# First two tiles of r and k by the sync queue in fp32, GpSimd's loads behind the masks, and another order: an RWKV-6 and mixture-of-adapters kernel

## The chip, the cores and the metric

One core of a Trainium2 chip runs the kernel. The metric is the device time of one execution in microseconds. Besides TensorE (PE, with its weight loads as PEld), the core has VectorE (DVE), ScalarE (ACT), GpSimd (POOL) and the sync engine (SP), and 16 DMA engines that all queues share. Each engine takes its instructions strictly in the order in which the program lists them.

## The reference

Two stages. A recurrence over 768 steps for 4 sequences of 8 heads with 48 features, then for each of the 3,072 rows a mixture of 8 low-rank adapters, of which the two with the largest logits count.

```
for t in range(S):
    cur = einsum('bhd,bhe->bhde', u * k[t], v[t])
    y[t] = einsum('bhd,bhde->bhe', r[t], state + cur)
    state = w[t][..., None] * state + einsum('bhd,bhe->bhde', k[t], v[t])

logits = x @ w_gate                      # x = y as (3072, 384)
top 2 of 8 experts, softmax over the two
out = x + sum over the two of weight * ((x @ A[e]) @ B[e])
```

## The kernel before

Work is cut into 24 tiles of 128 steps, six to each sequence; all 8 heads (384 columns) of a tile go together. Within a tile the recurrence is written as matrix products. A triangular matmul adds up log w (`cs`, `ci`), two exponentials turn the sums into factors (`grow`, `exps`), `mult` scales r and k by them, `tr` transposes both on PE, `trev` takes the result out of PSUM, `amm` forms the 128 x 128 products of r and k for each head, and `aev` masks them. `kv` adds to the state, which `sev` copies out. `ymm` makes the tile's output from state and masked products. The direct term of u is made apart: `rkp` multiplies r by k, `xk` and `xkev` transpose that (together with the output of a tile three earlier), `dgmm` and `dgev` give one number for each head and row, and `dv` multiplies v by it. `xev` adds `dv` and `ymm`'s result.

The second stage works in batches of four tiles (the last ones are of three and one): `lgmm` and `gate` for the logits, `gmax`, `gsel` and `gmul` for the weights, `zmm`, `zw`, `zT` and `zTev` for the low-rank middle, and for each tile `dmm`, `oev` and `store`. The name with a number, as in `mult.0`, is a stage and its tile; `xk.-3` is one that holds `rkp.0` alone.

The order is written out by hand in the string `ORDER` (lines 36 to 76): a list of stage and tile, which fixes the sequence of every engine's queue. Each stage's engine is fixed as well, or picked for each tile by the strings in `ENGINES` (lines 79 to 87: A is ACT, D is DVE, P is GpSimd; the string of `xkev` begins with tile -3).

Loads go by two queues. The sync queue carries w (in fp32: tile 0 and tile 1 apart, then pairs of tiles), the packed weights, the adapters' B, r and k of tile 0 in fp32 (`rk_first`), and the stores. The GpSimd queue carries the rest of r and k (`load_rk`, in groups of 1, 2 or 4 tiles) and v (`load_v`), and turns them into fp16 on the way. GpSimd also makes the masks: `strict` and the identity in `begin()`, `rest` and `at_mask` in `masks` (line 243). `rest` is first used by `cs.1`, `at_mask` by `aev.0`. `warm` issues matmuls whose result isn't used.

The engines' queues around the start, as `ORDER` gives them (before):

```
SP    w.0 rk.0 | w.1 weights moe_B w.2 w.4 w.6 ...
POOL  strict identity | rk.1 rk.2 v.0 v.1 rk.4 rk.6 masks v.4 rk.8 v.8 rk.12 v.12 dv.0 ...
ACT   ln.0 grow.0 exps.0 xkev.-3 ln1.0 cast16 grow.1 trev.0 xkev.-2 casts ...
DVE   rkp.0 rkp.1 mult.0 rkp.2 rkp.3 aev.0 mult.1 sev.0 xev.0 mult.2 aev.1 ...
```

Of the kernel before, what the change touches and what calls it, by code (L numbers as in the profile page):

```python
# [41 lines left out]
xkev.0 grow.3 dgmm.3 lgmm.0 aev.1 ci.3 sev.1 trev.2 ymm.1 exps.3 kv.2 cs.4 amm.2 ln.6 sev.2 xev.1 mult.3 tr.3 aev.2
kv.3 sev.3 dgev.3 grow.4 rkp.4 trev.3 ci.4 load_w.14 rkp.5 ymm.2 exps.4 ln.8 cs.5 amm.3 xk.1 grow.5 ci.5 mult.4 tr.4
xkev.1 dv.2 aev.3 exps.5 dgmm.4 ymm.3 cs.6 xev.2 ln.10 dv.3 rkp.6 load_w.16 grow.6 trev.4 mult.5 rkp.7 xk.2 xev.3
ci.6 amm.4 xkev.2 tr.5 xk.3 exps.6 cs.7 trev.5 load_v.16 aev.4 xkev.3 grow.7 amm.5 dgmm.5 lgmm.1 lgmm.2 dgmm.6
lgmm.3 ci.7 mult.6 tr.6 exps.7 aev.5 mult.7 trev.6 ymm.4 kv.4 cs.8 tr.7 amm.6 gate.3 grow.8 ln.12 ci.8 sev.4 ymm.5
exps.8 load_v.20 dgev.5 dv.4 trev.7 gmax.3 dv.5 xev.4 kv.6 cs.9 xk.4 gsel.3 aev.6 gmul.3 xev.5 zmm.3 grow.9 xkev.4
ci.9 amm.7 lgmm.4 dgmm.7 exps.9 cs.10 zw.3 rkp.8 dgev.7 rkp.9 mult.8 xk.5 sev.6 zT.3 dv.6 xkev.5 ymm.6 zTev.3
grow.10 tr.8 trev.8 aev.7 dv.7 dgmm.8 xev.6 dmm.0 ci.10 lgmm.5 kv.7 amm.8 ymm.7 xk.6 rkp.10 aev.8 xev.7 mult.9 oev.0
sev.7 store.0 ln.14 load_w.18 dmm.1 xkev.6 exps.10 kv.8 cs.11 xk.7 rkp.11 tr.9 mult.10 rkp.12 oev.1 grow.11 xkev.7  # L50
dgmm.9 ymm.8 ci.11 lgmm.6 lgmm.7 trev.9 exps.11 dgmm.10 gate.7 dgev.9 amm.9 tr.10 cs.12 sev.8 dmm.2 kv.9 aev.9
rkp.13 ln.16 dv.8 trev.10 sev.9 xev.8 gmax.7 mult.11 gsel.7 ymm.9 xk.8 dv.9 rkp.14 amm.10 gmul.7 kv.10 tr.11 xev.9
grow.12 ci.12 oev.2 xkev.8 aev.10 zmm.7 trev.11 zw.7 xk.9 exps.12 dmm.3 lgmm.8 dgmm.11 store.1 cs.13 amm.11 ymm.10
oev.3 xkev.9 zT.7 grow.13 sev.10 dgev.11 mult.12 tr.12 ci.13 lgmm.9 zTev.7 dgmm.12 rkp.15 kv.12 dmm.4 store.2
load_w.20 dv.10 aev.11 store.3 exps.13 cs.14 xev.10 ymm.11 dv.11 trev.12 oev.4 mult.13 xk.10 xev.11 dmm.5 grow.14
amm.12 ci.14 tr.13 store.4 ln.18 rkp.16 xkev.10 xk.11 lgmm.10 aev.12 exps.14 dgmm.13 mult.14 dgev.13 cs.15 trev.13
sev.12 ymm.12 dv.12 amm.13 oev.5 tr.14 kv.13 grow.15 xkev.11 lgmm.11 ci.15 dmm.6 trev.14 aev.13 gate.11 exps.15
amm.14 cs.16 rkp.17 sev.13 grow.16 xev.12 oev.6 xk.12 gmax.11 mult.15 zmm.11 gsel.11 aev.14 store.5 dv.13 ci.16
xkev.12 gmul.11 dgmm.14 tr.15 ymm.13 dgmm.15 dmm.7 kv.14 lgmm.12 ln.20 exps.16 trev.15 cs.17 dgev.15 zw.11 zT.11
store.6 amm.15 mult.16 xev.13 tr.16 oev.7 grow.17 sev.14 load_w.22 ci.17 zTev.11 rkp.18 xk.13 dv.14 exps.17 dv.15  # L60
rkp.19 xkev.13 trev.16 dmm.8 ymm.14 aev.15 cs.18 dgmm.16 oev.8 lgmm.13 grow.18 kv.15 amm.16 xev.14 ln.22 ci.18 xk.14
ymm.15 xkev.14 mult.17 aev.16 xev.15 dmm.9 tr.17 dmm.10 sev.15 dgmm.17 lgmm.14 exps.18 kv.16 trev.17 sev.16 cs.19
ymm.16 oev.9 mult.18 oev.10 grow.19 dgev.17 amm.17 ci.19 aev.17 rkp.20 dv.16 xev.16 xk.15 tr.18 exps.19 mult.19
rkp.21 xkev.15 cs.20 kv.18 xk.16 lgmm.15 dgmm.18 trev.18 grow.20 ymm.17 gate.15 ci.20 tr.19 xkev.16 dgmm.19 amm.18
gmax.15 dv.17 rkp.22 xev.17 exps.20 trev.19 gsel.15 gmul.15 dgev.19 mult.20 zmm.15 cs.21 sev.18 dv.18 grow.21 xk.17
store.7 lgmm.16 rkp.23 xkev.17 store.8 dmm.11 aev.18 kv.19 amm.19 lgmm.17 zw.15 sev.19 ci.21 zT.15 oev.11 exps.21
ymm.18 tr.20 dgmm.20 aev.19 zTev.15 dv.19 cs.22 dmm.12 trev.20 xev.18 ymm.19 dmm.13 amm.20 kv.20 mult.21 oev.12
grow.22 ci.22 oev.13 exps.22 xk.18 tr.21 xkev.18 xev.19 trev.21 xk.19 aev.20 cs.23 mult.22 store.9 dgmm.21 dgev.21
xkev.19 amm.21 dv.20 grow.23 sev.20 tr.22 store.10 lgmm.18 store.11 ymm.20 trev.22 ci.23 dmm.14 exps.23 oev.14
lgmm.19 aev.21 kv.21 amm.22 dmm.15 dv.21 gate.19 sev.21 xev.20 mult.23 store.12 xk.20 oev.15 xkev.20 gmax.19 aev.22  # L70
ymm.21 tr.23 dgmm.22 zmm.19 lgmm.20 dgmm.23 trev.23 kv.22 amm.23 gsel.19 sev.22 xev.21 xk.21 gmul.19 ymm.22 dgev.23
# [495 lines left out]
```

## Time and profile before

| what | value |
|---|---|
| median of 3 runs | 100.42 us (99.06 to 101.35) |
| the profiled execution | 100.22 us |
| its span in the profile | 98.5 us |
| PE busy, share of the span | 82.8 us, 84% |
| DVE busy | 79.0 us, 80% |
| ACT busy | 69.0 us, 70% |
| POOL busy | 49.2 us, 50% |
| moved by the GpSimd queue (loads) | 6.88 MB written, 41.7% of 16 engines' span |
| moved by the sync queue (loads and stores) | 10.25 MB, 31.5% |

The span runs from the first to the last instruction of one profiled execution; what lies around it belongs to the time as well. A row of the timeline gives start, duration, engine, line, operation, output and inputs with shapes, a count where neighbours were merged, and in brackets the idle time of the engine just before and what ended it. Busy time is what the profile shows as running; a matmul's end is modelled, and a PE that is busy all the time is not PE at its peak.

### The profile page before, as it was taken

The page shows a single profiled execution, that of the slowest core. Times are in us where ns is not written, and L with a number is a line of the kernel's source. Part 1 is how long each engine was busy: PE and PEld are TensorE (multiplying, and loading weights), DVE is VectorE, ACT ScalarE, POOL GpSimd, SP SyncE. Part 2 cuts the span into 40 slices and gives each one's busy share as a digit, 9 for nine tenths or more (in the row PEclk, how much of TensorE's full clock was granted, in tenths as well). Part 3 has the DMA queues.
Part 4 walks back from the last instruction along what each step waited for, and adds up shares of the span by engine and source line. Part 5 has one row for each costly group of instructions (what it writes and reads, how often), then busy time and mean ns, then how long its engine had stood idle before and what let it go on. Part 6 is the DMA issues. An engine that isn't in the chain of part 4 may idle for free.

```text
span 98.5 us, 3274 instructions
## 1 busy us (share of the span) xinstructions
PE 82.8 (84%) x1326; PEld 60.6 (62%) x1326; DVE 79.0 (80%) x165; ACT 69.0 (70%) x162; POOL 49.2 (50%) x77
## 2 busy tenths in 40 slices
PE   3871778897678998899998989999999999989730
PEld 2230536575356876767885867788787687957310
DVE  5514227679999989899999999999989999986610
ACT  5433346777957797879886978899886779655450
POOL 6997144600970087926757364773639306070100
PEclk9998555599999999999999999999999999999998
DMA  2999999999999999999999313522400240402644
GB/s 60 259 195 234 272 277 260 261 270 271 264 253 215 209 205 213 208 210 251 271 223 307 137 48 114 164 80 87 160 7 0 80 156 10 160 10 80 237 166 159
DMA packets 13439, 17.34 MB, mean 176 GB/s; under 512 B 880, under 2 KB 13296, under 8 KB 13424
## 3 DMA queue, kind: packets, MB, share of 16 engines
q0 software_dynamic: 6256, 6.88, 41.7%
q1 hardware_dynamic: 7168, 10.25, 31.5%
q8 instruction: 10, 0.16, 0.7%
q14 instruction: 5, 0.04, 0.1%
HBM read 19.29 MB, written 4.72 MB: 244 GB/s over the span
## 4 chain that ended last, share of the span: by engine, by line
PE 48%; DVE 25%; issue 7%; DMA 7%; ACT 5%; POOL 2%; ACTq 1%; POOLq 0%; DVEq 0%
PE trp L331 10%; DVE at L352 7%; DMA rk<-in_rk_dram 7%; PE xk_ps L398 6%; PE a_ps L346 5%; DVE rk L297 5%; DVE xs L389 4%; PE s_ps L363 3%; PE y_ps L383 3%; PE d_ps L496 3%; PE cs_ps L280 3%; PE cs_ps L289 3%; DVE zw L470 3%; PE cs_ps L281 3%; PE y_ps L377 2%
## 5 line engine op out<-in xcount | busy, mean ns | idle before, releaser
L322 POOL TENSOR_TENSOR dv<-v,dg 128x384 f32<-128x384 f16 x24 | 20.3, 862 | 22.7 <-DVE dg L255 11.5
L352 DVE TENSOR_TENSOR at<-a_ps,at_mask 128x1024 f16<-128x1024 f32 x24 | 29.2, 1216 | 2.4 <-PE a_ps L346 2.2
L331 PE MATMUL trp<-ident,rk 128*128 128x128 bf16 x192 | 15.6, 227 | 2.8 <-DVE rk L297 2.8
L285 ACT ACTIVATE e<-cs_ps 128x384 bf16<-128x384 f32 x24 | 12.0, 499 | 6.7 <-PE cs_ps L281 5.5
L305 POOL TENSOR_TENSOR rkp<-rk 128x384 f16<-128x384 f16 x14 | 13.3, 954 | 6.4 <-PE xk_ps L398 3.7
L331 PEld LDWEIGHTS <-rk 128*128 128x128 bf16 x192 | 12.2, 101 | 5.4 <-DVE rk L297 4.1
L297 DVE TENSOR_TENSOR rk<-rk,e 128x768 bf16<-128x768 f16 x23 | 14.5, 630 | 1.0 <-ACT e L293 1.0
L259 ACT COPY rkT<-trp 128x512 f32<-128x512 f32 x22 | 13.0, 591 | 2.1 <-PE trp L331 2.1
L293 ACT ACTIVATE e<-cs_ps 128x384 bf16<-128x384 f32 x24 | 11.8, 493 | 3.8 <-PE cs_ps L289 3.6
L389 DVE TENSOR_TENSOR xs<-dv,y_ps 128x384 f16<-128x384 f32 x24 | 13.1, 544 | 0.7 <-POOL dv L322 0.6
L259 ACT COPY xkT<-xk_ps 128x384 f32<-128x384 f32 (+1 forms) x25 | 11.2, 450 | 3.3 <-PE xk_ps L398 3.1
L346 PE MATMUL a_ps<-rkT 48*128 48x128 bf16 x192 | 10.0, 225 | 0.5 <-ACT rkT L259 0.3
L398 PE MATMUL xk_ps<-ident,rkp 128*128 128x128 f16 x72 | 8.4, 228 | 2.3 <-DVE rkp L305 2.3
L268 ACT ACTIVATE logw<-w_in 128x768 f16<-128x768 f32 x11 | 9.3, 848 | 0.0
L383 PE MATMUL y_ps<-v,at 128*128 128x48 f16 x192 | 8.8, 185 | 0.6 <-DVE at L352 0.6
L346 PEld LDWEIGHTS <-rkT 48*128 48x128 bf16 x192 | 5.9, 97 | 4.9 <-issue 1.5
L289 PE MATMUL cs_ps<-logw,ident 128*128 128x384 f16 x24 | 8.3, 346 | 0.5 <-ACT e L285 0.5
L281 PE MATMUL cs_ps<-logw,strict 128*128 128x384 f16 x24 | 8.3, 348 | 0.2 <-ACT logw L266 0.2
L398 PE MATMUL xk_ps<-ident,xs 128*128 128x128 f16 x72 | 8.2, 223 | 0.4 <-DVE xs L389 0.4
L253 ACT CAST S_sb<-s_ps 128x384 bf16<-128x384 f32 x15 | 7.4, 490 | 1.5 <-DVE dg L255 0.5
L496 PE MATMUL d_ps<-Ball,zT 128*128 128x384 f16 x24 | 7.8, 326 | 0.6 <-ACT zT L259 0.6
L502 ACT COPY res<-d_ps 128x384 f32<-128x384 f32 x13 | 6.1, 485 | 2.5 <-PE d_ps L496 2.3
(74 smaller groups left out, 158.6 us busy)
## 6 DMA issues: line engine op xcount, KB each, us to landing
out_dram<-res SPq DMA_DIRECT2D x24, 192.0 KB, 2.1
w_in<-in_w_dram SPq DMA_DIRECT2D x11, 384.0 KB, 14.1
...
v<-in_v_dram POOLq DMA_DIRECT2D x1, 288.0 KB, 12.1
```

The lines of the kernel that those rows point to most:

```text
L259: nc.scalar.copy(out=out.bitcast(F32), in_=in_.bitcast(F32))
L285: nc.scalar.activation(out=e2[:, 0], in_=cs_ps[:, 0:HD], func=ACT.Exp)
L293: nc.scalar.activation(out=st[t]["e2"][:, 1], in_=cs_ps[:, 0:HD], func=ACT.Exp, scale=-1.0)
L297: nc.vector.tensor_mul(rk2.rearrange("s m p h d -> s (m p h) d")[:, :, 0:D], st[t]["rk"].rearrange("s m (h d) -> s (m h) d", d=D), st[t][" ...
L305: (nc.gpsimd if ENGINES["rkp"][t] == "P" else nc.vector).tensor_mul(p_, st[t]["rk"][:, 0], st[t]["rk"][:, 1])
L322: nc.gpsimd.tensor_mul(dv_, st[t]["v16"], st[t]["dg"].rearrange("p (h o) -> p h o", o=1).to_broadcast([L, H, D]))
L331: nc.tensor.transpose(trp[:, m, p, :], rk2[:, m, p, :, :].rearrange("s a b -> s (a b)"), ident)
L346: nc.tensor.matmul(a_ps[:, g, p, :], lhsT=rkT[base:base + D, 1, p, :], rhs=rkT[base:base + D, 0, p, :], start=True, stop=True)
L352: nc.vector.tensor_mul(at, st[t]["a_ps"].rearrange("s g p f -> s (g p) f"), at_mask.to_broadcast([128, H, 128]))
L383: nc.tensor.matmul(y_ps[:, h, :], lhsT=d["at"][:, g * P + p, :], rhs=d["v16"][:, h, :], start=(c == 0 and h == 0), stop=(h == H - 1), skip ...
L389: nc.vector.tensor_add(xs, st[t]["dv"].rearrange("p a b -> p (a b)"), st[t]["y_ps"].rearrange("p a b -> p (a b)"))
L398: nc.tensor.transpose(xk_ps[:, 3 * q + j, :], src[:, j * 128:(j + 1) * 128], ident16)
```

## The change

Tile 1 of r and k joins tile 0 in a constant fp32 buffer, `rk_first`, and comes by the sync queue, behind the weights. GpSimd's first load is now v of tile 0, then come the masks, then r and k of tiles 2 and 3. `ORDER` is replaced as a whole, with the same 642 items but for `load_rkf.1` in place of `load_rk.1`. The strings that pick engines change too: on DVE, `oev` runs for 16 tiles instead of 11, `dgev` for 6 instead of 3, `xkev` for 3 instead of 2, `zTev` for one batch instead of none, `sev` for 3 instead of 5, `rkp` for 7 instead of 10 (the other three go to GpSimd). Where `oev` runs on DVE, `dmm` needs one matmul instead of two.

```diff
-RKGROUPS = {0: 1, 1: 1, 2: 2, 4: 2, 6: 2, 8: 4, 12: 4, 16: 4, 20: 4}
-RKBUFS = {1: 1, 2: 3, 4: 4}
+RKGROUPS = {2: 2, 4: 2, 6: 2, 8: 4, 12: 4, 16: 4, 20: 4}
+RKBUFS = {2: 3, 4: 4}
+HW_RK = 2
...
-warm.0 load_w1.0 load_wsb.0 load_rk.1 load_rk.2 adapters.0 load_v.0 load_w.2 load_v.1 load_rk.4 load_w.4 ln.0
-load_rk.6 masks.0 load_v.4 load_rk.8 load_v.8 rkp.0 load_w.6 cs.0 rkp.1 grow.0 load_w.8 warm.1 load_w.10 ci.0 warm.2
...
+warm.0 rkp.0 load_w1.0 ln.0 load_wsb.0 cs.0 grow.0 warm.1 xk.-3 ci.0 ln1.0 xkev.-3 exps.0 load_rkf.1 load_w.2
+adapters.0 warm.2 load_v.0 masks.0 cs.1 load_rk.2 load_w.4 mult.0 load_v.1 tr.0 trev.0 grow.1 cast16.0 ci.1 dgmm.0
+amm.0 kv.0 rkp.1 load_rk.4 exps.1 xk.-2 xkev.-2 mult.1 load_rk.6 load_v.4 load_w.6 aev.0 dgmm.1 sev.0 dgev.1
...
-    trev="AADADAAAAAAAAAAAAAAAAAAA",
-    xkev="AAAAAAAAADAAAAAAAAAAAAAAADA",
-    out="AAADDDDDDDDDDAAAAAAADAAA",
-    sev="DDADDAAAAAAAAAAAAAAADAAA",
-    rkp="DDDDDDPDPDPPDPPPPPPPPDPP",
-    dgev="AAADADAAAAAAADAAAAAAAAAA",
-    zTev="DDDADDDADDDADDDADDDADDAA",
+    trev="DADAAAAAAAAAAAAAAAAAAAAA",
+    xkev="DAAAADDAAAAAAAAAAAAAAAAAAAA",
+    out="ADDDDDDDDADDDAAADADADDDA",
+    sev="DDADAAAAAAAAAAAAAAAAAAAA",
+    rkp="DDDDPDPPDPPPPPPPPPPPPDPP",
+    dgev="AAADAAADAAADADAAADAAADAA",
+    zTev="DDDDDDDADDDADDDADDDADDAA",
...
+    rk_first = const.tile([L, HW_RK, 2, HD], F32, name="rk_first")
+
+    def load_rkf(t):
+        nc.sync.dma_start(out=rk_first[:, t], in_=rk[t])
+        st[t]["rk"] = rk_first[:, t]
+
     def load_rk(t):
         n = RKGROUPS[t]
-        if t == 0:
-            rk_in = const.tile([L, 1, 2, HD], F32, name="rk_first")
-            nc.sync.dma_start(out=rk_in[:, 0], in_=rk[t])
-        else:
...
     def begin():
         load_w(0)
-        load_rk(0)
+        load_rkf(0)
```

The same queues by the new `ORDER`:

```
SP    w.0 rk.0 | w.1 weights rk.1 w.2 moe_B w.4 w.6 ...
POOL  strict identity | v.0 masks rk.2 v.1 rk.4 rk.6 v.4 rk.8 rk.12 v.8 dv.0 v.12 dv.1 ...
ACT   ln.0 grow.0 ln1.0 exps.0 grow.1 cast16 exps.1 xkev.-2 dgev.1 trev.1 ln.2 xkev.-1 grow.2 xkev.0 exps.2 ...
DVE   rkp.0 xkev.-3 mult.0 trev.0 rkp.1 mult.1 aev.0 sev.0 rkp.2 rkp.3 xev.0 aev.1 dgev.3 mult.2 sev.1 trev.2 ...
```

On PE, `xk.-3` now stands ahead of `ci.0`, `cs.1` ahead of `tr.0`, `xk.0` between `cs.2` and `ci.2`, and `ymm.23` ahead of `xk.22`. On ACT, `ln.4` to `ln.10` each stand behind the `grow` of the next tile where they stood ahead of it.

More of the change, by code (lines that the diff above doesn't have):

```diff
@@ L42 @@
[L42 to L71, printed above, removed]
@@ new lines @@
+grow.16 kv.13 amm.14 gate.11 xev.12 dv.13 sev.13 xk.12 oev.6 ci.16 zmm.11 xkev.12 lgmm.12 dgmm.15 kv.14 gmax.11
+exps.16 ln.20 sev.14 mult.15 tr.15 cs.17 ymm.13 dmm.7 kv.15 gsel.11 rkp.17 aev.14 trev.15 amm.15 grow.17 ci.17
+gmul.11 zw.11 dgev.15 mult.16 zT.11 store.5 xev.13 sev.15 exps.17 zTev.11 load_w.22 tr.16 xk.13 rkp.18 dv.14 oev.7
+ymm.14 dmm.8 cs.18 trev.16 aev.15 xkev.13 kv.16 amm.16 lgmm.13 ln.22 dmm.9 dgmm.16 oev.8 xev.14 grow.18 xk.14 dv.15
+mult.17 ci.18 rkp.19 ymm.15 oev.9 tr.17 aev.16 xkev.14 rkp.20 exps.18 xev.15 dgmm.17 trev.17 dmm.10 store.6 cs.19
@@ L76 @@
+xk.23 gsel.22 dmm.18 xkev.23 gmul.22 oev.18 zmm.22 lgmm.23 gate.23 dmm.19 zmm.23 oev.19 zw.22 store.10 gmax.23 zT.22
+store.11 zTev.22 gsel.23 zw.23 dmm.20 zT.23 dmm.21 oev.20 oev.21 dmm.22 zTev.23 oev.22 store.12 store.13 store.14
+dmm.23 store.15 store.16 store.17 store.18 store.19 oev.23 store.20 store.21 store.22 store.23
 """
```

47 lines of the change are left out of this document (35 added, 12 removed).

## The prediction

> **What bounds the kernel now.** I began with the busy time by stretches of the span: for each stretch its length, then busy microseconds and instruction counts of PE, PEld, DVE, ACT and POOL, then granted clock, DMA share and GB/s.
>
> ```profile
> 22.20:87.00 64.80, 60.99 (x1121) 47.60 (x1116) 62.72 (x127) 52.72 (x127) 34.27 (x47) 1.00 0.71 164
> 0.00:8.92 8.92, 4.77 (x18) 2.15 (x18) 3.44 (x11) 3.63 (x6) 7.64 (x21) 1.00 0.80 180
> 8.92:22.20 13.28, 10.88 (x130) 7.33 (x131) 7.54 (x13) 7.96 (x18) 5.31 (x7) 0.61 1.15 267
> 87.00:98.50 11.50, 6.15 (x71) 3.52 (x67) 5.31 (x18) 4.73 (x14) 1.97 (x4) 0.98 0.38 138
> ```
>
> From 22.2 to 87 us DVE is busy 62.72 of 64.80 us and PE 60.99: here work sets the pace, and only work taken off both engines shortens it. The first 22.2 us are another regime: DVE works 11 us of them, the DMA engines are full from about 9 us on, and PE's clock averages 0.61 in the second stretch. The last 11.5 us are a chain of short steps. So I read the start next, first on the chain of waits, then on DVE.
>
> ```profile
> 1.83 6.79 DMA rk<-in_rk_dram
> ...
> 9.93 1.03 PE trp L331 x8
> ```
>
> ```profile
> 4.79 0.56 DVE L305 TENSOR_TENSOR rkp<-rk_first 128x384 f16<-128x384 f32 x1 [1.03 <-DMA rk_first<-in_rk_dram]
> 8.64 0.36 DVE L305 TENSOR_TENSOR rkp<-rk 128x384 f16<-128x384 f16 x1 [3.30 <-DMA rk<-in_rk_dram]
> 8.92 0.95 DVE L297 TENSOR_TENSOR rk<-rk_first,e 128x768 bf16<-128x768 f32 x1
> 11.63 0.63 DVE L305 TENSOR_TENSOR rkp<-rk 128x384 f16<-128x384 f16 x2 [1.76 <-DMA rk<-in_rk_dram]
> 14.12 1.23 DVE L352 TENSOR_TENSOR at<-a_ps,at_mask 128x1024 f16<-128x1024 f32 x1 [1.86 <-PE a_ps L346]
> ```
>
> The chain's first 6.8 us are the load of r and k of tile 1, yet tile 1 is not what the engines need first. DVE's queue holds rkp.1 ahead of mult.0, so tile 0 waits behind tile 1's data for 3.30 us. What mult.0 itself needs is older, as ACT's timeline shows: exps.0 (the 5.38 row) had ended at 5.87.
>
> ```profile
> 5.38 0.49 ACT L293 ACTIVATE e<-cs_ps 128x384 bf16<-128x384 f32 x1 [0.57 <-PE cs_ps L289]
> 6.80 0.32 ACT L259 COPY xkT<-xk_ps 128x192 f32<-128x192 f32 x1 [0.93 <-PE xk_ps L398]
> 7.91 0.52 ACT L273 ACTIVATE logw<-w_in 128x384 f16<-128x384 f32 x1 [0.79 <-DMA w_in<-in_w_dram]
> 9.45 0.55 ACT L517 CAST w<-w_sb 128x432 f16<-128x432 f32 x1 [1.01 <-DMA w_sb<-in_weights_dram]
> ```
>
> **The start, part 1: when data lands.** The new order puts mult.0 ahead of rkp.1, but it also puts ln1.0, which needs the second tile of w, ahead of exps.0 on ACT, and rkp.1 and mult.1 ahead of aev.0 on DVE. So three landings on the sync queue now matter: w1, then rk.1 as fp32 (384 KB, behind the weights), then the w pairs. Their price comes from the steps between landings. rk_first was in at about 4.8, w1 at 7.9 (3.1 us for 192 KB, beside rk.1 and rk.2 of the GpSimd queue), the weights at 9.45 (1.5 us for 216 KB). The next rows are two w pairs: issue time, then time to landing.
>
> ```profile
> L165 SPq DMA_DIRECT2D w_in<-in_w_dram x1: 434/434/434, 3.1 to 3.1; - x1
> DMA to landing us min/median/max: 10.0/10.0/10.0
> L165 SPq DMA_DIRECT2D w_in<-in_w_dram x1: 962/962/962, 5.8 to 5.8; - x1
> DMA to landing us min/median/max: 15.6/15.6/15.6
> ```
>
> The pair w.2 landed at 13.1: 3.65 us behind the weights, for itself and the 192 KB of moe_B between, so 1.2 us per 192 KB. Pair w.8 landed at 21.4.
>
> After: while w1 moves, GpSimd's queue holds only v.0, half of rk.1's bytes, and then pauses for the masks.
>
> ```profile
> 5.95 0.24 POOL masks.py:101 MEMSET rest<- 128x128 f16 x1
> ...
> 7.01 0.76 POOL L188 DMA_DIRECT2D v<-in_v_dram  x1
> ```
>
> The four mask instructions take 1.06 us and one DMA issue 0.76, so rk.2 is issued at 1.83 + 0.76 + 1.06 = 3.65 instead of some 2.6. w1 lands 1.2 to 3.1 us behind 4.8. I take 1.7, close to the weights' step, so 6.5. Weights: 8.0. rk.1: two 192 KB steps of 1.2 at the least, two of 3.1 at the most. I take 2.5, the weights' rate to within 0.2, so 10.5. That is later than its 8.64 of before, and it stands in a place where that hurts less. Then w.2 lands at 13.0, as before, and all later pairs come after moe_B, 1.1 us later than before: w.8 at 22.5. The GpSimd loads behind rk.2 have one transfer fewer ahead of them, and I charge them nothing.
>
> **The start, part 2: the chain.** ln1.0 at 6.5 takes 0.52, exps.0 0.49, so mult.0 starts at 7.5 (8.92 before) and ends at 8.45. tr.0 at its 1.03 ends at 9.5. trev.0 is now on DVE (0.68, row below): 10.2. rkp.1 waits for 10.5, takes 0.56 from fp32; mult.1 from fp32 takes 0.95 instead of 0.55. aev.0 starts at 12.0, against 14.12. Both masks, made by 3.65, cost nothing, as their users start after 6. Then DVE runs aev.0 1.23, sev.0 0.56, rkp.2 and 3 0.63, xev.0 0.56, to 15.0. mult.2 now stands behind exps.2, which stands behind xkev.0 on ACT and xk.0 on PE: 0.4 + 0.5 + 0.5 (an estimate from the rows of the same operations above), 16.4. Two rows of DVE say where before was then.
>
> ```profile
> 18.44 0.56 DVE L297 TENSOR_TENSOR rk<-rk,e 128x768 bf16<-128x768 f16 x1 [0.96 <-ACT e L293]
> ```
>
> ```profile
> 22.74 1.22 DVE L352 TENSOR_TENSOR at<-a_ps,at_mask 128x1024 f16<-128x1024 f32 x1
> ```
>
> From mult.2 to aev.2 took 4.3 us before, aev.1 among it. In the new order aev.1 runs before mult.2, in its wait, so 3.1 remain: aev.2 at 19.5, a gain of 3.2.
>
> What is late next is the w stream. ln.8 now comes behind grow.5 on ACT:
>
> ```profile
> 25.16 0.48 ACT L285 ACTIVATE e<-cs_ps 128x384 bf16<-128x384 f32 x1
> ```
>
> Less 3.2 that is wanted at 22.4, and w.8 comes at 22.5; exps.5 is queued behind it. So the start gives 3.0 us. With w1 at 7.9 and rk.1 at 12.1 it gives about 1.4; with w1 at 6.0 some 3.6.
>
> **The middle.** Between tiles 4 and 21, DVE's list changes by: evacuations oev.1 and 2 come and oev.9 goes; sev.4 and 20 go; rkp.4, 7, 9 and 12 go (to GpSimd) and rkp.8 comes; trev.4 goes; xkev.2 and 3 come and 6 goes; three dgev come; zTev.3 comes.
>
> ```profile
> L504 DVE TENSOR_TENSOR res<-d_ps,xs 128x384 f32<-128x384 f32 x10 | 5.5, 550 | 0.1
> L305 POOL TENSOR_TENSOR rkp<-rk x14: 908/912/1223, 26.3 to 75.4; 128x384 f16<-128x384 f16 x14
> L305 DVE TENSOR_TENSOR rkp<-rk x9: 343/352/982, 8.6 to 71.8; 128x384 f16<-128x384 f16 x9
> L255 DVE CAST S_sb<-s_ps x5: 546/558/558, 16.0 to 81.2; 128x384 bf16<-128x384 f32 x5
> L255 DVE COPY dg<-s_ps x3: 161/165/168, 24.3 to 57.3; 128x16 f32<-128x16 f32 x3
> L261 DVE COPY rkT<-trp x2: 678/680/681, 21.2 to 28.3; 128x1024 bf16<-128x1024 bf16 x2
> L261 DVE COPY xkT<-xk_ps x2: 358/454/551, 43.7 to 89.2; 128x768 f16<-128x768 f16 x1, 128x384 f16<-128x384 f16 x1
> ```
>
> 0.55 - 1.12 - 3 x 0.35 - 0.68 + 0.55 + 0.50 + 0.4 (zTev, between the two copies of the last row) = -0.85 us. PE, nearly as full, loses only the identity matmuls of two outputs and gains one. The three rkp that go to GpSimd there add 3 x 0.91 us of its time, which its idle half hides; but a DVE rkp took 0.35 or 0.98, so something stretches DVE by up to 0.63 at times, and if each of the three does so, 1.9 comes back. So the middle is worth -0.85 to +1.0; I take -0.5, nearer the counted end. w.18, w.20 and w.22 now stand behind other stores on the sync queue; the worst is w.20, behind store.4:
>
> ```profile
> 54.15 0.56 DVE L504 TENSOR_TENSOR res<-d_ps,xs 128x384 f32<-128x384 f32 x1
> 61.10 0.86 ACT L268 ACTIVATE logw<-w_in 128x768 f16<-128x768 f32 x1
> ```
>
> oev.4 ends 6.4 us ahead of ln.20: free, unless a landing takes over 6 us.
>
> **The tail.** oev.16, 18, 21 and 22 go from ACT to DVE, which is idle half the last stretch.
>
> ```profile
> 93.64 0.48 ACT L502 COPY res<-d_ps 128x384 f32<-128x384 f32 x1 [0.75 <-PE d_ps L496]
> 94.02 0.22 ACT L259 COPY zT<-zT_ps 128x64 f32<-128x64 f32 x1
> 94.69 0.86 ACT L502 COPY res<-d_ps 128x384 f32<-128x384 f32 x2 [0.46 <-PE d_ps L496]
> ```
>
> ```profile
> 93.44 0.22 PE L480 MATMUL zT_ps<-ident,zw 128*128 128x128 f16 x1
> ```
>
> zTev.23 waited for oev.21 on ACT, though zT.23 was done at 93.66. Now it runs at 93.7 to 93.9, dmm.23 about 0.5 later, oev.23 0.48 more: 94.9 against 95.55, -0.65 (0 to -0.8).
>
> **Sum.** The profiled execution took 100.22 us (span 98.5 and 1.72 around it), 0.2 below the median of the runs shown. 100.22 - 3.0 - 0.5 - 0.65 = 96.1.
>
> **The rivals.**
> (a) The loads keep half of the start. w1 at 7.9 and rk.1 at 12.1: start -1.4, middle 0, tail -0.65, 98.2 us. For it: the only w1 on record took 3.1 us. Against: rk.1 and rk.2 ran beside that one.
> (b) Slower: the sync queue gets a small share once rk.2 runs beside it. If rk.1 takes two steps of 3.1 behind the weights, it lands at 7.9 + 1.5 + 6.2 = 15.6, aev.0 starts at 17.1, 3.0 later than before, and nothing behind it on DVE can run. With the tail at -0.65 that is 102.6 us. The point from which it decides is a landing of rk.1 after 12.6, where aev.0 is back at 14.12. Against it: the steps of 1.5 and 1.2 were also beside rk.2. The Trainium skill (DMA: Bandwidth & Descriptors, Queues, rings and completion order) states that each engine takes turns between the queues it has work for, packet by packet. By that the fp32 rows of rk.1 would wait one turn of rk.2's for each of theirs, which is this rival's cause; the trace bears the sharing out in the 3.1 us of w1, and shows with 1.5 and 1.2 that turns alone needn't cost so much.
> (c) PE's clock stays full.
>
> ```profile
> 9.06 0.41 PE L398 MATMUL xk_ps<-ident,rkp 128*128 128x128 f16 x3 [2.29 <-DVE rkp L305]
> ```
>
> Before, PE stood idle 2.3 us there, and the stretch from 8.92 on averaged 0.61. With mult.0 earlier and warm.2 right ahead of cs.1, tr.0 could run in 0.5 instead of 1.03, and the other PE steps up to mult.2 save about 1 more: 94.6 us. Against: PE still waits for trev.0, rk.1 and aev.0. The Trainium skill (TensorE: Matmul & The Clock Gate, Part 1) puts the halving after an idle window of about 3.4 us; by that this rival would be the likelier, since no gap of mine is that long, but before lost its clock behind shorter gaps too.
> (d) The middle gives it back: new waits between queues of 0.15 us a tile over 21 tiles, 99.2 us. For it: DVE and PE are both near full and every item was moved. Against: GpSimd and ACT, which feed them, have room.
>
> **Chances.** Forecast 0.45, (a) 0.17, (b) 0.13, (c) 0.13, (d) 0.12. 2% of the median is 2.0 us, about what a measurement of this kernel can tell from no change, so faster means below 98.4. Faster: forecast 0.44, (c) 0.13, half of (a) 0.09: 0.66. Same: the other half of (a), (d) and 0.01: 0.21. Slower: (b) 0.13. The forecast's own range is 94.7 to 98.3 (start -1.7 to -3.6, middle and tail at their ends in part). The range 93.9 to 100.6 takes in (a), (c) and (d) and leaves out (b).
>
> **What would show it.** mult.0 before 8 us with exps.0 as its releaser, and rkp.1 no longer ahead of it; aev.0 near 12, aev.2 near 19.5; little or no ACT wait before ln.8; DVE as full as before from there on; zTev.23 not behind an output copy. Wrong if DVE waits over 1.5 us for rk.1, if ACT waits for w in several places, or if the stretch from aev.2 to the tail grows.

## The result, and the profile after

| | median | executions | ratio to the kernel before |
|---|---|---|---|
| before | 99.83 us | 20, 98.67 to 101.35 | |
| changed | 98.69 us | 20, 97.59 to 100.51 | 0.987 [0.983, 0.992] |

The change gains 1.3%, where 4.1% were forecast: 98.69 us instead of 96.1. Here and in the table below, medians are of all executions, while a ratio compares only those within 1.5% of the shortest of their kernel and is missing where too few were left, so it can differ from the ratio of the medians. The profiled execution of the changed kernel is one of its longer ones, 99.81 us, with a span of 98.1; the shortest, 97.59 us, had a span of 95.9.

The busy time by stretches says where the gain is and where it goes. The stretches are cut at the starts of `aev.2`, `aev.12`, `aev.13` and `aev.23`; the columns are the stretch, its length, busy time and counts of PE, PEld, DVE, ACT and POOL, then granted clock, DMA share and GB/s. First the kernel before, then the changed one.

```profile
22.74:55.68 32.94, 29.93 (x528) 22.54 (x529) 31.75 (x61) 25.98 (x60) 18.67 (x24) 1.00 1.14 232
55.68:57.83 2.15, 2.15 (x43) 1.76 (x42) 2.15 (x4) 1.64 (x5) 0.76 (x2) 1.00 0.22 80
57.83:87.06 29.23, 28.75 (x549) 23.32 (x546) 28.34 (x63) 24.62 (x63) 14.91 (x23) 1.00 0.26 91
87.06:98.50 11.44, 6.09 (x69) 3.46 (x64) 5.25 (x18) 4.67 (x14) 1.91 (x4) 0.98 0.38 138
```

```profile
10.27:20.45 10.18, 8.16 (x97) 5.17 (x97) 7.11 (x14) 6.00 (x13) 5.63 (x7) 0.68 1.14 264
20.45:52.28 31.83, 30.09 (x527) 22.30 (x527) 30.36 (x60) 25.79 (x56) 19.73 (x26) 0.99 1.19 236
52.28:57.34 5.06, 3.05 (x32) 2.09 (x32) 1.85 (x4) 3.92 (x8) 1.80 (x3) 0.76 0.80 258
57.34:85.97 28.63, 28.57 (x546) 23.08 (x545) 27.70 (x62) 23.95 (x58) 14.64 (x22) 0.98 0.20 71
85.97:98.10 12.13, 5.71 (x71) 3.60 (x71) 6.70 (x21) 3.66 (x12) 1.47 (x4) 0.91 0.36 132
```

`aev.2` comes 2.3 us earlier (20.45 against 22.74), and by `aev.12` the changed kernel is 3.4 us ahead. Then one step between two tiles takes 5.06 us where it took 2.15, with VectorE (DVE) busy for 1.85 of them, and 2.9 us are gone. The tail takes 0.7 us more. So -2.3 -1.1 +2.9 -0.6 +0.7 = -0.4 us between the two spans.

What stands in the long step is plain on ScalarE's timeline, and the sync queue's shows why. The first row is the start's `ln1.0`, the second `ln.18`:

```profile
5.35 0.52 ACT L278 ACTIVATE logw<-w_in 128x384 f16<-128x384 f32 x1 [0.60 <-DMA w_in<-in_w_dram]
53.02 0.84 ACT L273 ACTIVATE logw<-w_in 128x768 f16<-128x768 f32 x1 [2.99 <-DMA w_in<-in_w_dram]
```

```profile
41.15 3.16 SPq L513 DMA_DIRECT2D out_dram<-res  x2
44.36 1.20 SPq L168 DMA_DIRECT2D w_in<-in_w_dram  x1
45.65 5.67 SPq L513 DMA_DIRECT2D out_dram<-res  x3
```

The chain of waits runs through the same place: store.1, the load of w.18 (w of tiles 18 and 19) behind it, then ScalarE.

```profile
43.95 0.36 SPq L513
44.36 8.64 DMA w_in<-in_w_dram
53.05 0.72 issue
53.77 0.48 ACT e L298
```

w.18 is issued at 44.36, since the sync queue waited for the output copies that the stores before it need, and it lands 8.6 us later, at 53.0. `exps.14` is queued behind `ln.18` on ScalarE, and `mult.14` and `tr.14` need it, so VectorE and PE stand still too. In the kernel before, w.18 stood behind store.0 only, was issued at 41.79 and landed 8.2 us later; `ln.18` ran at 54.86, and nobody waited.

The start, on VectorE:

```profile
6.41 0.96 DVE L302 TENSOR_TENSOR rk<-rk_first,e 128x768 bf16<-128x768 f32 x1 [0.48 <-ACT e L298]
8.93 0.55 DVE L310 TENSOR_TENSOR rkp<-rk_first 128x384 f16<-128x384 f32 x1
10.27 1.22 DVE L357 TENSOR_TENSOR at<-a_ps,at_mask 128x1024 f16<-128x1024 f32 x1
12.93 0.63 DVE L310 TENSOR_TENSOR rkp<-rk 128x384 f16<-128x384 f16 x2 [0.98 <-DMA rk<-in_rk_dram]
```

`mult.0` starts at 6.41 with `exps.0` as its releaser, `rkp.1` (8.93) waits for no load, and `aev.0` comes at 10.27, 3.9 us earlier than before. But `rkp.2` now waits 0.98 us for rk.2, and from about 14 to 20 us PE runs at about half clock. The page's rows of PE's clock and of the DMA engines' busy share, in tenths for 40 slices of 2.45 us, show both that and what w.18 met:

```profile
PEclk9999985579999999999999669999999999999995
DMA  2999999999999999999999902024200140403580
```

The two sixes of the clock lie just behind the wait for w.18. The DMA engines are full from the second slice to the 23rd, that is to about 56 us; GpSimd's large loads among the work are issued some 26 us ahead of their landing.

### The profile page after: what moved, and what is told of

The parts are those of the page before. It is cut to its first block, busy times and chain, and to the rows that moved or that the text cites. A ratio compares the mean times of both kernels' runs of the same rounds, so it can differ in the third digit from the quotient of the medians.

```text
span 98.1 us, 3275 instructions
## 1 busy us (share of the span) xinstructions
PE 83.4 (85%) x1321; PEld 60.2 (61%) x1321; DVE 80.1 (82%) x170; ACT 68.0 (69%) x154; POOL 51.9 (53%) x79
## 4 chain that ended last, share of the span: by engine, by line
PE 49%; DMA 18%; DVE 14%; ACT 5%; issue 4%; POOL 3%; POOLq 0%; SPq 0%; DVEq 0%; ACTq 0%
DMA rk<-in_rk_dram 9%; DMA w_in<-in_w_dram 9%; PE trp L336 9%; PE xk_ps L403 6%; PE a_ps L351 5%; DVE at L357 5%; PE y_ps L388 4%; PE s_ps L368 4%; PE cs_ps L285 3%; PE cs_ps L294 3%; PE d_ps L501 3%; PE cs_ps L286 3%; PE y_ps L382 2%; DVE rk L302 2%; PE z_ps L460 2%
## 5 line engine op out<-in xcount | busy, mean ns | idle before, releaser
L310 POOL TENSOR_TENSOR rkp<-rk 128x384 f16<-128x384 f16 x17 | 16.1, 949 | 4.7 <-PE xk_ps L403 2.5
L258 ACT CAST S_sb<-s_ps 128x384 bf16<-128x384 f32 x17 | 8.2, 481 | 1.6 <-PE s_ps L368 1.4
L285 PE MATMUL cs_ps<-logw,rest 128*128 128x384 f16 x20 | 6.8, 341 | 2.8 <-ACT e L298 2.8
L452 POOL TENSOR_TENSOR ge<-ge,den 128x32 f32<-128x32 f32 (+1 forms) x6 | 1.9, 310 | 13.2 <-DVE g L447 10.3
L509 DVE TENSOR_TENSOR res<-d_ps,xs 128x384 f32<-128x384 f32 x16 | 8.5, 548 | 0.1
```

What stands on the lines that cost most here:

```text
L310: (nc.gpsimd if ENGINES["rkp"][t] == "P" else nc.vector).tensor_mul(p_, st[t]["rk"][:, 0], st[t]["rk"][:, 1])
```

## The experiments

"w.18 early" is the changed kernel with that one load moved. All medians, with the kernel before on the same chip:

| kernel | this | before | ratio |
|---|---|---|---|
| w.18 early, three times | 96.14, 97.39, 96.35 | 99.80, 99.87, 99.52 | 0.965 [0.959, 0.971], none, 0.968 [0.959, 0.977] |
| before, w.18 early | 99.93 | 99.80 | 1.009 [1.002, 1.017] |
| changed, once more | 98.69 | 99.87 | none |
| changed, w.18 behind store.3 | 101.89 | 99.52 | 1.023 [1.014, 1.032] |
| changed, v.20 later | 98.58 | 100.36 | 0.992 [0.985, 0.998] |
| w.18 early, `rkp` as before | 98.30 | 100.36 | 0.991 [0.987, 0.996] |
| w.18 early, all letters as before | 101.34 | 100.36 | 1.022 [1.016, 1.028] |
| w.18 early, last copies on ACT, twice | 95.58, 96.54 | 100.36, 99.52 | 0.963 [0.959, 0.968], 0.961 [0.953, 0.969] |
| w.18 early, rk.1 by GpSimd, twice | 96.38, 96.56 | 99.80, 99.87 | 0.955 [0.949, 0.961], none |
| w.18 early, rk.2 ahead of masks | 96.77 | 99.87 | none |
| before, `mult.0` ahead of `rkp.1` | 99.67 | 99.80 | none |

### Where w.18 stands

The theory was that the place of w.18 behind store.1 loses what the start gains. The first kernel issues it with the loads of the start, ahead of all stores.

```diff
-xev.6 load_w.16
+xev.6 load_w.16 load_w.18
...
-store.1 oev.4 load_w.18 mult.13
+store.1 oev.4 mult.13
```

> The changed kernel with the load of w for tiles 18 and 19 moved ahead of store.0 on the sync queue, and nothing else. Theory A (the start's gain arrived and was lost at ln.18, which waited 3.0 us for a pair of w that stood behind store.1 and took 8.6 us to land): the wait goes, aev.13 starts at about 54.4 instead of 57.3, and the time falls by 2.5 to 3.5 us, to 0.955 to 0.965 of before. Theory B (the stretch around 50 us is held by the GpSimd loads or by PE and DVE work, and the wait only shows it): ln.18 no longer waits, something else does, and the time stays within 0.7 us of the changed kernel, 0.98 to 0.99 of before.

The control does the same to the kernel before, where nobody waits for w.18.

```diff
-rkp.6 load_w.16 grow.6
+rkp.6 load_w.16 load_w.18 grow.6
...
-store.0 ln.14 load_w.18 dmm.1
+store.0 ln.14 dmm.1
```

> The kernel before with the same one load moved ahead of store.0. Theory A: no wait of ACT for w past tile 1 shows in before, so its time stays, 0.995 to 1.005. Rival: an earlier pair of w helps any order (or hurts it, by taking DMA time from the GpSimd loads), and the ratio leaves that band.

96.14 us against 99.80, as theory A had it, so this version beats both kernels. The kernel before gains nothing, 99.93 us; by the ratio that is 0.9% more, outside the 0.995 to 1.005 that was expected. Its trace differs from the one of the kernel before only ahead of `aev.2` (24.71 against 22.74); between `aev.12` and `aev.13` it takes 2.16 us as before. Whether the earlier load or the execution made its start slower is not shown. The stretches of the changed kernel with w.18 early, in the same columns and cut at the same places to within 0.04 us:

```profile
11.50:20.00 8.50, 6.28 (x98) 3.83 (x97) 7.17 (x14) 6.20 (x14) 5.63 (x7) 1.00 1.15 266
20.00:51.30 31.30, 29.89 (x531) 22.50 (x532) 30.00 (x60) 27.58 (x60) 20.04 (x26) 1.00 1.18 236
51.30:53.00 1.70, 1.61 (x31) 1.21 (x29) 1.70 (x4) 1.65 (x4) 0.61 (x2) 1.00 1.19 288
53.00:81.34 28.34, 28.24 (x546) 22.71 (x546) 27.68 (x64) 24.24 (x59) 15.91 (x23) 1.00 0.31 111
81.34:93.50 12.16, 5.71 (x71) 3.60 (x71) 6.66 (x21) 3.61 (x12) 1.43 (x4) 0.91 0.36 131
```

The step of 5.06 us is 1.70 us here, and the terms against the kernel before are -2.7 (start), -1.6, -0.5, -0.9 and +0.7, together -5.0 us of span. This execution also had PE's full clock from 11.5 to 20 us, which the changed kernel's had not. The two other traces of w.18 early had a low clock at the start; there `aev.2` came at 21.26 and 19.88, and the long step took 1.70 and 1.71 us.

The changed kernel itself ran again, and w.18 early beside it on the same chip, both without a further edit.

> The changed kernel as it is, on the same chip as the kernel with w.18 early, for a second trace and a direct difference. Theory store (w.18 behind store.1 is what the change loses): the trace shows ScalarE waiting 1.5 to 3 us for w_in ahead of ln.18 again, and the kernel is 2.0 to 3.0 us slower than the one with w.18 early. Theory luck (the wait of 2.99 us was that one execution's): the wait is under 1 us and the difference under 1.5 us.

> The kernel with w.18 early once more, on one chip with the three others, as what they are compared with: 95.2 to 96.9 us, ratio to the kernel before 0.96 to 0.97, no wait ahead of ln.18. Should PE's clock halve somewhere between 11 and 22 us in its trace, as in all traces but two so far, aev.2 comes at 21 to 22 instead of 20.0 and the time is 1.1 us above that of an execution with the full clock.

98.69 against 97.39: 1.3 us, and the trace had no wait ahead of `ln.18`. Both are what the theory of luck expected: the wait of 2.99 us is not in every execution. The kernel with w.18 early, too, came out above the 95.2 to 96.9 expected of it. The rows say more. The sync queue issues w.18 at 47.79, ScalarE takes it at 53.34 without a wait, and the view of the tile `w_in` gives the landing (start window 47 to 49):

```profile
47.79 1.13 SPq L168 DMA_DIRECT2D w_in<-in_w_dram  x1
```

```profile
DMA to landing us min/median/max: 5.2/5.2/5.2
```

```profile
53.34 0.84 ACT L273 ACTIVATE logw<-w_in 128x768 f16<-128x768 f32 x1
```

47.8 + 5.2 = 53.0, as 44.36 + 8.6 was. In this execution the start and the first tiles ran slower (w.1 was there at 7.00 instead of 5.35, PE's clock averaged 0.60 from 27 to 30 us, and `aev.12` came at 55.70 instead of 52.28), so ScalarE came to `ln.18` when the load was there; and `aev.13` followed in the usual 1.70 us, at 57.40, against 57.34 in the trace with the wait. The two times agree, but they are no floor of the kernel. From `aev.13` to the end of the span the traces of the changed kernel and of w.18 early take 40.3 to 40.8 us, so the shortest execution of the changed kernel, with its span of 95.9, was there at 55.1 to 55.6. What does hold is that a good start is lost where w.18 lands later than ScalarE wants it. Two runs try what sets the landing.

```diff
-store.1 oev.4 load_w.18 mult.13 dv.11 rkp.15 ln.18 store.2 xev.11 exps.14 oev.5 sev.12 store.3 xk.10
+store.1 oev.4 store.2 store.3 load_w.18 mult.13 dv.11 rkp.15 ln.18 xev.11 exps.14 oev.5 sev.12 xk.10
```

> The changed kernel with the loss made larger: stores 2 and 3 stand ahead of w.18 as well, so w.18 is issued behind store.3, at about 49.3 where the changed kernel's first trace had 44.36. Theory floor (w.18 lands when the 16 DMA engines are through with all the loads, at 53.0 in both traces of the changed kernel, whether it was issued at 44.36 or 47.79): it lands at 53 to 54, ln.18 starts there, aev.13 at 57.3 to 58.5, time within 1 us of the changed kernel's 98.69. Theory queue (a landing takes 8 us from its issue in this stretch): it lands at 57 to 58, aev.13 near 62, time 102 to 103.

The landing came out nearer to the floor theory, the time (101.89 us) nearer to the queue theory. The sync queue and ScalarE:

```profile
49.52 0.43 SPq L168 DMA_DIRECT2D w_in<-in_w_dram  x1
```

```profile
54.85 0.84 ACT L273 ACTIVATE logw<-w_in 128x768 f16<-128x768 f32 x1 [4.62 <-DMA w_in<-in_w_dram]
```

Issued 5.2 us later than in the first trace, the load lands 1.8 us later; 5.3 us are left from issue to landing, as the 5.2 of the second trace. So in these three traces w.18 landed at 53.0 or some 5.2 us behind its issue, whichever was later. The time, 101.89 us, is 3.2 above the changed kernel: making the wait larger makes the loss larger.

The other run leaves w.18 where the change has it and takes bytes off the engines ahead of it.

```diff
-tr.7 load_v.20 ci.8
+tr.7 ci.8
...
-dv.11 rkp.15
+dv.11 load_v.20 rkp.15
```

> The changed kernel with w.18 where the change has it, behind store.1, but GpSimd's load of v.20 (384 KB as fp16, 768 KB read) issued behind dv.11 instead of behind dv.5. Theory full engines (w.18 takes 8.6 us because GpSimd's loads, issued some 25 us ahead of their landing, fill the DMA engines up to 53 us): the engines have 3 to 4 us less to move by then, w.18 lands by 50, ScalarE's wait of 2.99 us ahead of ln.18 falls under 0.7, time 96 to 97. Theory queue (w.18 is slow because of the stores around it on the sync queue): landing 8 us again, the wait stays at 2 to 3 us, time 98.7 within 0.5.

ScalarE, VectorE and GpSimd:

```profile
50.48 0.84 ACT L273 ACTIVATE logw<-w_in 128x768 f16<-128x768 f32 x1 [0.49 <-DMA w_in<-in_w_dram]
```

```profile
50.84 2.23 DVE L302 TENSOR_TENSOR rk<-rk,e 128x768 bf16<-128x768 f16 x1
```

```profile
50.86 1.79 POOL L310 TENSOR_TENSOR rkp<-rk 128x384 f16<-128x384 f16 x2
```

w.18, issued at 44.32, was there at 50.5 instead of 53.0, and the wait fell from 2.99 to 0.49 us, as the theory of the full engines had it. The time did not follow, 98.58 us: what the wait gave back was lost one step earlier. GpSimd spends 0.81 us on issuing v.20 just there, so its two `rkp` come back to back, and `mult.13` beside them takes 2.23 us instead of 0.55. From `aev.11` to `aev.12` it takes 5.14 us, against 3.46 or 3.47 in the traces of the changed kernel and of w.18 early. `aev.13` came at 55.63, 1.7 us earlier than in the first trace of the changed kernel. That the medians show nothing of it would follow if a usual execution of the changed kernel loses at `ln.18` about as much as this step costs, 1.7 us; both its traces are of longer executions (99.81 and 99.44 us), so this is not shown.

### The middle

With w.18 early, `aev.2` to `aev.23` takes 61.35 us in the first trace, 3.0 less than the 64.32 before, where the prediction had 0.5. Two runs take back letters, on the order of w.18 early. First `rkp` alone, then every letter of tiles 4 to 20:

```diff
-    rkp="DDDDPDPPDPPPPPPPPPPPPDPP",
+    rkp="DDDDDDPDPDPPDPPPPPPPPDPP",
```

> The kernel with w.18 early, with before's letters for rkp from tile 4 on: rkp.4, 7, 9 and 12 on VectorE again, rkp.8 on GpSimd. In the kernel with w.18 early aev.2 to aev.23 takes 61.35 us against 64.32 in the kernel before, 3.0 less where the prediction had 0.5. Theory list (a shorter VectorE list, each instruction at its own 0.35 us): 3 x 0.35 = 1.05 us comes back, aev.2 to aev.23 about 62.4, time near 97.1. Theory collision (rkp on VectorE beside GpSimd's rkp and dv is stretched to 0.9 us, and others with it): 2 to 3 us comes back, VectorE's mean rkp back at 0.45 or more, aev.2 to aev.23 63.4 to 64.4, time 98 to 99. Theory order (the sequence alone brings the gain): under 0.4 us comes back, time 96.1 to 96.5.

```diff
-    trev="DADAAAAAAAAAAAAAAAAAAAAA",
-    xkev="DAAAADDAAAAAAAAAAAAAAAAAAAA",
-    out="ADDDDDDDDADDDAAADADADDDA",
-    sev="DDADAAAAAAAAAAAAAAAAAAAA",
-    rkp="DDDDPDPPDPPPPPPPPPPPPDPP",
-    dgev="AAADAAADAAADADAAADAAADAA",
-    zTev="DDDDDDDADDDADDDADDDADDAA",
+    trev="DADADAAAAAAAAAAAAAAAAAAA",
+    xkev="DAAAADDAADAAAAAAAAAAAAAAAAA",
+    out="ADDDDDDDDDDDDAAAAAAADDDA",
+    sev="DDADDAAAAAAAAAAAAAAADAAA",
+    rkp="DDDDDDPDPDPPDPPPPPPPPDPP",
+    dgev="AAADADAAAAAAADAAAAAAADAA",
+    zTev="DDDADDDADDDADDDADDDADDAA",
```

> The kernel with w.18 early, with before's letters for tiles 4 to 20 in every string (rkp, out, sev, trev, xkev, dgev, and zTev for batches that end in tile 4 to 19); the order stays. Theory list: 0.85 us more VectorE work in the middle, aev.2 to aev.23 about 62.2, time near 97. Theory collision: as with rkp alone, 63.4 to 64.4, time 98 to 99. Theory order: 61.4 to 61.8, time 96.1 to 96.6. A stretch of over 64.5 would mean that order and letters only fit together.

The stretch from `aev.2` to `aev.23`, in the columns used above: the kernel before, w.18 early, `rkp` as before, all letters as before.

```profile
22.74:87.06 64.32, 60.83 (x1115) 47.62 (x1115) 62.24 (x126) 52.24 (x125) 34.34 (x47) 1.00 0.71 163
```

```profile
19.99:81.34 61.35, 59.74 (x1101) 46.42 (x1101) 59.39 (x126) 53.48 (x122) 36.58 (x49) 1.00 0.78 180
```

```profile
21.72:84.39 62.67, 59.79 (x1102) 46.47 (x1101) 59.95 (x128) 53.15 (x122) 33.18 (x45) 1.00 0.75 169
```

```profile
22.18:88.22 66.04, 60.49 (x1101) 47.03 (x1100) 61.98 (x131) 51.66 (x120) 32.73 (x45) 0.99 0.69 158
```

The first steps of this stretch are no clean measure. `aev.2` to `aev.5` takes 8.40, 9.76 and 9.10 us in the three traces of w.18 early, whose clocks differ there, and the whole stretch 61.35, 62.60 and 61.97. From `aev.5` to `aev.23` the traces of one kernel agree: 55.27 us before, 52.91, 52.84 and 52.87 with w.18 early, 53.99 with `rkp` as before, 56.31 with all letters as before. So from there on the new order and letters gain 2.4 us, and `rkp` alone gives back 1.1. That is the number of the list theory (1.05), but the mechanism of the collision theory: 0.9 of it lies in the step from `aev.9` to `aev.10` (5.61 against 4.70), where one `rkp` on VectorE is stretched beside two `dv` of GpSimd (43.87 to 45.61 us):

```profile
43.94 0.98 DVE L310 TENSOR_TENSOR rkp<-rk 128x384 f16<-128x384 f16 x1
```

The time, 98.30 us, fits the collision theory too (98 to 99); it is 2.7 us above the 95.58 of the run with the last copies on ScalarE on the same chip, and where the part beyond 1.1 comes from is open. All letters give back 3.4 us from `aev.5` on, more than the whole gain: in the new order before's letters make VectorE wait for other engines (66.04 - 61.98 = 4.1 us idle in the whole stretch, against 2.0). So the new order without its letters holds no gain; the new letters on the old order were not run.

VectorE's own busy time in the whole stretch fell by 62.24 - 59.39 = 2.85 us (3.0 and 2.1 in the two other traces) where its list counted 0.85. The groups by line show what the count missed; first the kernel before, then w.18 early:

```profile
L305 DVE TENSOR_TENSOR rkp<-rk 128x384 f16<-128x384 f16 x9 | 3.6, 420 | 5.1 <-DMA rk<-in_rk_dram 5.1
L442 DVE TENSOR_TENSOR g<-ge,top 128x32 f32<-128x32 f32 (+1 forms) x6 | 1.9, 323 | 0.0
```

```profile
L310 DVE TENSOR_TENSOR rkp<-rk 128x384 f16<-128x384 f16 x5 | 1.7, 351 | 0.0
L447 DVE TENSOR_TENSOR g<-ge,top 128x32 f32<-128x32 f32 (+1 forms) x6 | 1.1, 179 | 0.0
```

The `rkp` cost 420 ns each and now 351; of the 1.9 us that the group lost, 0.36 is `rkp.1`, which now reads `rk_first`, so 1.5 us belong to the middle. `gsel`, of which nothing was changed but its place, fell from 323 to 179 ns, 0.8 us in all. That makes 2.3 us where the count had 1.05 for `rkp` and nothing for `gsel`.

### The tail

```diff
-    out="ADDDDDDDDADDDAAADADADDDA",
+    out="ADDDDDDDDADDDAAAAAAADAAA",
```

> The kernel with w.18 early, with the output copies of tiles 16, 18, 21 and 22 back on ScalarE as before (each with the second matmul that this takes). The prediction gave the tail 0.65 us for moving them. Theory tail (the move gained it): last output copy ends 0.5 to 0.8 us later counted from aev.23, time 96.6 to 96.9. Theory drain (what the last copies gain is lost again, since the last stores come closer together and stay behind one another on the sync queue: from the end of the last copy to the end of the span it took 4.3 us there and 2.95 before): last copy 0.5 to 0.8 later, but the rest shorter by as much, time 96.1 within 0.3.

> The kernel with w.18 early and the output copies of tiles 16, 18, 21 and 22 on ScalarE, once more, now on one chip with the kernel it differs from. Theory tail (the move to VectorE gained 0.65 us): 0.4 to 0.9 us slower than that kernel. Theory drain (the last copy comes 0.4 us later, but the time from it to the end of the span is as much shorter): from aev.23 to the end of the span 11.8 us again, against 12.0 to 12.2 there, and 0 to 0.5 us faster.

> The kernel with w.18 early, as the one that the two others of this chip are compared with: 95.2 to 98.2 us with a median of 96.1 to 97.4, aev.23 to the end of the span 12.0 to 12.2 us, w.18 issued with the first loads and never waited for.

The second and third ran on one chip. From `aev.23` to the end of the span, the copies on ScalarE (11.84 us the other time), then w.18 early:

```profile
83.88:95.70 11.82, 6.30 (x75) 3.97 (x75) 4.93 (x17) 5.32 (x16) 1.47 (x4) 1.00 0.37 135
```

```profile
81.85:94.10 12.25, 5.71 (x71) 3.60 (x71) 6.70 (x21) 3.67 (x12) 1.47 (x4) 0.94 0.36 130
```

With the copies on VectorE the stretch is 0.4 us longer, not shorter, as the theory of the drain had it; the medians differ by 0.2 us the other way, 96.54 and 96.35, which is no difference. The move to VectorE gains nothing in the time.

### The start

The part that names the change, r and k of tile 1 by the sync queue, is undone here: they come by GpSimd as fp16 again, as its first load.

```diff
-RKGROUPS = {2: 2, 4: 2, 6: 2, 8: 4, 12: 4, 16: 4, 20: 4}
-RKBUFS = {2: 3, 4: 4}
-HW_RK = 2
+RKGROUPS = {1: 1, 2: 2, 4: 2, 6: 2, 8: 4, 12: 4, 16: 4, 20: 4}
+RKBUFS = {1: 1, 2: 3, 4: 4}
+HW_RK = 1
...
-exps.0 load_rkf.1 load_w.2 adapters.0 warm.2 load_v.0 masks.0
+exps.0 load_w.2 adapters.0 warm.2 load_rk.1 load_v.0 masks.0
```

> The kernel of the first run of this call, but r and k of tile 1 come by GpSimd in fp16 as its first load, ahead of v of tile 0. If the sync queue's fp32 load is worth its place (my sum), w1 lands at 7.9 again instead of 5.3, mult.0 starts near 9, rk.2 lands later, and the time is 2 to 3 us above the first run of this call. If only the order of DVE's queue matters, rk.1 lands near 8.6, where rkp.1 now stands anyway, and the time is within 0.7 us of it.

> The kernel with w.18 early, but r and k of tile 1 by GpSimd as fp16, as its first load, as in the run with one look at it before; now with more rounds, beside the kernel with w.18 early on one chip. Theory sync queue (fp32 by the sync queue is worth something: w.1 landed 2.5 us earlier with it and aev.0 came 0.8 us earlier): 0.5 to 1.5 us slower than the kernel with w.18 early. Theory order (the order alone brings the start, and tile 2 is late in either way): within 0.3 us of it.

96.38 and 96.56 us, against 96.14 and 97.39 with the sync queue on the same chips: no difference that executions from 95.2 to 99.7 us can show, and not the loss that the theory of the sync queue asked for, 2 to 3 us and then 0.5 to 1.5. ScalarE and VectorE of the second show both sides:

```profile
7.55 0.52 ACT L278 ACTIVATE logw<-w_in 128x384 f16<-128x384 f32 x1 [2.71 <-DMA w_in<-in_w_dram]
```

```profile
8.49 0.96 DVE L302 TENSOR_TENSOR rk<-rk_first,e 128x768 bf16<-128x768 f32 x1 [2.55 <-ACT e L298]
10.77 0.35 DVE L310 TENSOR_TENSOR rkp<-rk 128x384 f16<-128x384 f16 x1
```

w.1 comes 2.2 us later than in the changed kernel (7.55 against 5.35), so `mult.0` does too; but from fp16 `rkp.1` takes 0.35 us instead of 0.55 and `mult.1` 0.55 instead of 0.95, and `aev.0` starts at 11.50.

The next run moves `mult.0` ahead of `rkp.1` in the kernel before, and does nothing else of the change.

```diff
-cs.0 rkp.1 grow.0
+cs.0 grow.0
...
-xkev.-3 xk.-2 mult.0 ln1.0 rkp.2 tr.0 cast16.0
+xkev.-3 mult.0 ln1.0 tr.0 rkp.1 xk.-2 rkp.2 cast16.0
```

> The kernel before with one thing of the new order: rkp.1 and xk.-2 stand behind mult.0 and tr.0. If that stall of 3.3 us was the cost, mult.0 starts near 6, aev.0 near 12.3 instead of 14.12, and the time falls by 1.5 to 2 us, 0.98 to 0.985 of before. If ln1.0, the weights and rk.2 end later than that stall anyway, aev.0 moves by less than 0.7 us and the ratio is 0.993 to 1.0.

```profile
5.84 0.96 DVE L297 TENSOR_TENSOR rk<-rk_first,e 128x768 bf16<-128x768 f32 x1 [0.74 <-ACT e L293]
9.56 0.36 DVE L305 TENSOR_TENSOR rkp<-rk 128x384 f16<-128x384 f16 x1 [2.77 <-DMA rk<-in_rk_dram]
12.53 0.63 DVE L305 TENSOR_TENSOR rkp<-rk 128x384 f16<-128x384 f16 x2 [2.61 <-DMA rk<-in_rk_dram]
```

`mult.0` starts at 5.84, 3.1 us earlier, and VectorE then waits 2.77 us for rk.1 and 2.61 for rk.2. `aev.0` came at 13.15, 1.0 us earlier and so between what the two theories expected, and `aev.2` at 22.59, against 22.74. Without the later items in another order the early `mult.0` is worth 0.15 us by `aev.2`, and nothing that shows in the time (99.67 against 99.80).

Last, rk.2, which `rkp.2` waited for in the changed kernel, ahead of the masks on GpSimd:

```diff
-load_v.0 masks.0 cs.1 load_rk.2
+load_v.0 load_rk.2 masks.0 cs.1
```

> The kernel with w.18 early, with GpSimd's load of rk.2 issued ahead of the four mask instructions, so 1.06 us earlier (at about 2.6 instead of 3.64). rkp.2 waited 0.98 us for rk.2 in the changed kernel. Theory late load (rk.2 sets the start from rkp.2 on): rkp.2 starts up to 1 us earlier and aev.2 with it, 0.5 to 1 us faster than the kernel with w.18 early. Theory shared engines (rk.2 then moves beside w.1, the weights and rk.1 and holds them up): w.1 lands after 5.6 and rk.1 after 8.4, aev.0 0.5 to 1.5 us later, time equal or up to 1 us slower.

```profile
10.67 0.56 DVE L310 TENSOR_TENSOR rkp<-rk_first 128x384 f16<-128x384 f32 x1 [1.34 <-DMA rk_first<-in_rk_dram]
```

Nobody waits for rk.2 any more, but rk.1 lands 8.0 us after its issue, where it took 5.7 to 6.6 in the traces of the changed kernel and of w.18 early, and `rkp.2` runs at 13.61: the engines were full, and one load was paid for with another, as the theory of the shared engines had it. 96.77 us against 97.39, within the spread of either.

## Why the prediction was right in sign and wrong in size

**The step that failed** is the sentence on the sync queue: "w.18, w.20 and w.22 now stand behind other stores on the sync queue; the worst is w.20, behind store.4 ... free, unless a landing takes over 6 us." The worst was w.18, behind store.1. By the rows of the kernel before it looked safer than w.20: `oev.1` had ended at 43.23 and `ln.18` ran at 54.86, 11.6 us apart, against 6.4 for w.20. But the slack has to be taken in the new order's times. There ScalarE came to `ln.18` at 50.03, 4.8 us earlier, and store.1 was no earlier than before, so w.18 was issued at 44.36 with 5.7 us left. And a landing did take over 6 us: 8.6, as w.18's had taken 8.2 in the kernel before. With fewer bytes of GpSimd's ahead it took 6.1 (v.20 later), so the full DMA engines are at least part of why. In that trace the step from `aev.12` to `aev.13` cost 3.4 us more (5.06 against 1.70 with the load moved). Over executions the loss is smaller: 1.3 us between medians on one chip, and about 2% by the ratios (0.987, and 0.965 and 0.968 with w.18 early).

That moving w.18 brings the medians to 96.14, 97.39 and 96.35, around the forecast of 96.1, is in part luck: the terms of the middle and the tail were off in opposite directions, and the sum had started from one execution of 100.22 us, 0.4 above the median of the twenty.

**The start** was forecast at -3.0 and gave -2.3 in the first trace and -1.3 in the second (`aev.2` at 20.45 and 21.48). In the first each landing on the sync queue was early: w.1 by 5.35 (6.5 forecast), rk.1 by 8.9 (10.5), and `aev.0` came at 10.27 (12.0); in the second w.1 was there at 7.00 and `aev.0` came at 12.75. In the first the lead was lost in two places. From `aev.0` to `mult.2` it took 5.83 us (4.4 forecast); the wait of `rkp.2` for rk.2 is in there, but `aev.0` to `aev.1` took 3.67 us with it and 3.41 in the trace of w.18 early without it, so it is worth 0.3. From `mult.2` to `aev.2` it took 4.35 us (3.1 forecast, and 3.28 in the trace of w.18 early that kept PE's full clock); other traces with a low clock have 3.98 and 4.44, but so has one with the full clock (3.99, rk.1 by GpSimd), so the clock as the cause is not shown. The w stream, named as late next at `ln.8`, made no one wait there. Rival (b), the sync queue starved by rk.2, did not occur: rk.1 landed 5.9 and 6.6 us after its issue at 2.6. The first term of the sum, rk.1 by the sync queue, was not needed for the gain: by GpSimd the time is the same.

**The middle** was mis-sized the safe way: -0.5 forecast, -1.7 to -3.0 in three traces without the wait, of which -2.4 from `aev.5` on in each. The count of the list took each instruction at its undisturbed 0.35 us; the stretched ones were the dear ones, and the feared return ("1.9 comes back") did not come. With the wait the stretch from `aev.2` to the tail grew, 65.52 us against 64.32, which the prediction had named as a sign of being wrong.

**The tail** was wrong in sign: -0.65 forecast, +0.7 in the trace. The last copy does end 0.6 us sooner after `aev.23` (93.85 - 85.97 = 7.9, against 95.55 - 87.06 = 8.5), as `zTev.23` no longer stands behind an output copy,

```profile
92.42 0.21 ACT L264 COPY zT<-zT_ps 128x64 f32<-128x64 f32 x1 [0.66 <-PE zT_ps L485]
...
93.37 0.48 ACT L507 COPY res<-d_ps 128x384 f32<-128x384 f32 x1 [0.73 <-PE d_ps L501]
```

but from there to the end of the span it takes 4.25 us instead of 2.95. The prediction ended its sum at the last copy, and the rest is no constant. What fills the added 1.3 us was not settled.

**The rivals.** (a), 98.2 us, and (d), 99.2, came equally near in time, but by other mechanisms: for (a) w.1 would have had to be late and the start to give 1.4 us, which only the second trace comes near to (w.1 at 7.00, -1.3), and for (d) there would have been waits spread over the tiles instead of one in one place. (c), PE's clock staying full, is no property of the change but of an execution: with w.18 early the granted clock went from 0.919 to 0.988 over 18 executions, those at 0.926 or less took 97.16 to 98.24 us, and of the five at 0.97 or more four took 95.16 to 95.70 and one 98.12.
